# Turns of x and of attention weights by 32-row groups beside products, and two shared h buffers in PSUM

## The chip, the cores and the metric

The kernel runs on one core of one Trainium2 chip. The metric is the device time in microseconds of one execution, as the median of several runs. The core's engines are TensorE (PE; its weight loads are listed apart as PEld), VectorE (DVE), ScalarE (ACT), GpSimd (POOL) and SyncE (SP), whose queue issues all the DMAs of this kernel. All data are 32-bit floats. A "record" is one line of the hardware profiler: a 32-bit product on PE leaves two, a 32-bit transpose one.

## The reference

Four batches of 12608 tokens with 128 channels go through two attention steps with 32 inducing points, and then, token by token, through a block of 1024 hidden units:

```python
I = np.broadcast_to(inducing[None], (B, m, C))          # B, N, m, C = 4, 12608, 32, 128
def mab(q, kv):
    s = scale * (q @ kv.transpose(0, 2, 1))
    s = s - s.max(-1, keepdims=True)
    a = np.exp(s)
    a /= a.sum(-1, keepdims=True) + 1e-09
    return a @ kv
h = mab(I, x)                                           # 32 rows per batch
attn = mab(x, h)                                        # 12608 rows per batch
# then for the 50432 rows x of attn:
h = x @ w_in                                            # 128 -> 1024
sm = np.exp(h - h.max(-1)) / (sum + 1e-09)
solu = h * sm
ln = (solu - mu) / np.sqrt(var + 1e-06) * g_ln
out = ln @ w_out                                        # 1024 -> 128
```

## The kernel before

A tile is 128 tokens; a batch has 99 (the last one half full), so there are 396 tiles in all. The program is written out in full by a planner in Python: generators (`p1`, `p2`, `main`, `soft` and others) hand it operations with a cost and a priority, and `Planner.run` picks the next one among the engines by numbers of its own (`BEAT`, `SWITCH`, `AFTER`, `SLACK`, the `PR_` constants). Buffers are `Lock` objects: a generator asks for one and gets it when an earlier user has given it back. What reaches the chip is a fixed list of instructions per engine, with waits between them.

**First pass, `p1(b, k)`.** Nine groups per batch, seven of 12 tiles, one of 8 and one of 7. A group loads x into `xn`, turns each tile on PE (L561: full 128x128 transposes against the identity, four to an operation, into a PSUM bank), copies the four to `xT` on ACT (L547), stores `xT` to `xd` in DRAM, and then computes the scores against the inducing points (L589), a running maximum by way of a small product (L614), the exponentials (L639), and the weighted sum of x (L665). For batch 0 this pass runs alone, ahead of everything, in "early" buffers; for batches 1 to 3 it runs inside the main work of the batch before.

**`combine(b)`** ends the pass with the 32 rows h (L707, L714) and multiplies them with `w_in` into `hs` (L726, copied by ACT at L728), so that the hidden layer of a tile is a product of the 32 attention weights of each token with `hs`.

**Second pass, `p2(b, j)`.** It loads `xT` back, makes the scores against h (L768), the row maxima, the exponentials and the row sums, doubles the 32 weights of a token to 64 columns (`a4`), and turns `a4` on PE (L804: full transposes of two tiles each, four to an operation), copied to `aT` by ACT (L812).

**`main` and `soft`.** A tile's hidden layer takes eight products with 32 contraction rows (L902), two row groups of the PE array at a time, into a PSUM buffer `h` of two banks. DVE scales it by the row sums and takes the maximum (L940), which frees `h`; ACT takes the exponential (L950); POOL multiplies (L954); ACT squares (L965); DVE turns the result in 32x32 blocks (L978) into `vt`. Four tiles make a group for the output product.

**Products.** The output product of a group (L1023) is 128 matmuls, 32 for each of the four row groups of the array; row groups 0 and 1 are pair 0, which writes to buffer `op0`, and row groups 2 and 3 are pair 1 with `op1`. The function `beats` writes them in steps, called beats, of one step for each pair that has products ready. While `main` uses one pair for L902, it calls `beats` for the other pair, so that products of both kinds run side by side in the array. The full-array operations (L561, L804 and all the scores) are not mixed with products.

**PSUM.** Of the eight banks, `h` has two, the two `op` buffers two each, `tr` one (the turns of both passes and the scores of the second), `pb` one (the scores and sums of the first pass).

The weights `w_in` and `w_out` arrive as 64-bit numbers and are rounded by DVE, ACT and POOL (`weights_in`, `weights_out`) during the first pass of batch 0. `w_out` is then spread to `wc` by 16 DMAs (L481).

## Time and profile before

| | |
|---|---|
| median of 3 runs | 1289.62 us (1284.67 to 1293.36) |
| the profiled execution, its own time | 1285.68 us |
| its span, first to last instruction | 1283.9 us |
| busy: PE / DVE / ACT / POOL | 1246.2 / 1140.8 / 1140.1 / 1104.2 us |
| mean granted TensorE clock | 0.992 of full speed |
| L1023 products of the output | 25600 records |
| L902 products of the hidden layer | 6336 records |

The busy time of PE comes from records whose ends are modelled and overlap one another, so a stretch of PE that is 98% busy need not be at its peak. Where a stretch of PE is read below, it is by the starts of its records.

### The profile page before, as it was taken

Reading aid. Unit: us, or ns where it says so; the run is one execution under the profiler, and the core shown is the slowest. Engines: PE = TensorE matmul, PEld = TensorE weight load, DVE = VectorE, ACT = ScalarE, POOL = GpSimd, SP = SyncE. Lnnn points to the kernel's source line nnn. Section 1 sums busy time; section 2 is a strip of 40 time slices with the busy share of each in tenths; the row PEclk is TensorE's granted clock in tenths of the full one; section 3 lists DMA queues with packets and bytes.
Section 4 is the critical chain, followed back from the end, with each engine's and each line's share of the span. In section 5 each row is a group of like instructions: output and inputs, shape, how many; then the busy total and the mean of one; then the engine's idle time right before and its main releaser. Section 6 shows DMA issues by size and latency. Waiting matters only on the chain.

```text
span 1283.9 us, 75837 instructions
## 1 busy us (share of the span) xinstructions
PE 1246.2 (97%) x34221; PEld 1120.8 (87%) x34221; DVE 1140.8 (89%) x1825; ACT 1140.1 (89%) x2418; POOL 1104.2 (86%) x981
## 2 busy tenths in 40 slices
PE   8899999999999999999999999999999999999996
PEld 6689888889888888889888998888989999999996
DVE  5589989999898989999888999899999999999993
ACT  5489999999889989999789999989988999999993
POOL 2388988889889988988888997978889999999994
PEclk9999999999999999999899999999999999999998
DMA  9652333331232233332133134233021211111111
GB/s 361 188 164 70 111 103 94 93 111 43 77 117 60 78 102 119 103 109 74 28 102 94 43 103 138 91 101 102 21 82 54 58 55 53 54 38 43 29 29 41
DMA packets 118149, 113.46 MB, mean 88 GB/s; under 512 B 76577, under 2 KB 83777, under 8 KB 117697
## 3 DMA queue, kind: packets, MB, share of 16 engines
q1 hardware_dynamic: 117824, 108.62, 27.6%
q8 instruction: 267, 4.37, 1.4%
q14 instruction: 58, 0.47, 0.1%
HBM read 54.30 MB, written 52.18 MB: 83 GB/s over the span
## 4 chain that ended last, share of the span: by engine, by line
PE 70%; DVE 3%; ACT 2%; issue 1%; POOL 1%; POOLq 0%; DVEq 0%; ACTq 0%
PE op L1023 46%; PE h L902 15%; PE tr L561 2%; PE tr L804 2%; PE tr L768 1%; PE pb L665 1%; PE pb L589 1%; ACT sq L965 1%; DVE spare L940 1%; DVE vt L978 1%; ACT eu L950 1%; POOL eu L954 1%; PE pb L726 0%; DVE hn L940 0%; PE pb L614 0%
## 5 line engine op out<-in xcount | busy, mean ns | idle before, releaser
L1023 PE MATMUL op<-wc,vt 32*128 32x129 f32 x25600 | 1007.7, 275 | 12.5 <-issue 8.4
L1023 PEld LDWEIGHTS op<-wc,vt 32*128 32x128 f32 x25600 | 945.4, 185 | 54.3 <-issue 39.8
L902 PE MATMUL h<-hs,aT 32*128 32x128 f32 x6336 | 442.8, 277 | 3.2 <-DVE spare L940 1.2
L902 PEld LDWEIGHTS h<-hs,aT 32*128 32x128 f32 x6336 | 387.9, 187 | 32.1 <-DVE spare L940 6.2
L954 POOL TENSOR_TENSOR eu<-spare,eu 128x1024 f32<-128x1024 f32 x144 | 341.2, 2376 | 33.8 <-ACT eu L950 33.4
L954 POOL TENSOR_TENSOR eu<-hn,eu 128x1024 f32<-128x1024 f32 x140 | 331.8, 2376 | 25.1 <-ACT eu L950 24.3
L978 DVE STREAM_TRANSPOSE vt<-eu 128x1024 f32<-128x1024 f32 x284 | 349.2, 1233 | 1.1 <-POOL eu L954 0.9
L965 ACT ACTIVATE sq<-eu 128x1024 bf16<-128x1024 f32 x284 | 298.9, 1053 | 17.2 <-POOL eu L954 13.7
L940 DVE TENSOR_SCALAR_CACHE_REDUCE hn<-h,rn 128x1024 f32<-128x1024 f32 x198 | 252.1, 1273 | 38.8 <-PE h L902 30.6
L940 DVE TENSOR_SCALAR_CACHE_REDUCE spare<-h,rn 128x1024 f32<-128x1024 f32 x198 | 251.8, 1272 | 37.2 <-PE h L902 28.2
L950 ACT ACTIVATE eu<-hn,nm 128x1024 f32<-128x1024 f32 x140 | 160.3, 1145 | 19.9 <-DVE hn L940 19.0
L950 ACT ACTIVATE eu<-spare,nm 128x1024 f32<-128x1024 f32 x144 | 164.9, 1145 | 10.7 <-DVE spare L940 10.5
L954 POOL TENSOR_TENSOR spare<-hn,spare 128x1024 f32<-128x1024 f32 x58 | 137.5, 2374 | 15.6 <-ACT spare L950 15.5
L954 POOL TENSOR_TENSOR spare<-spare 128x1024 f32<-128x1024 f32 x54 | 128.0, 2373 | 16.9 <-ACT spare L950 16.4
L978 DVE STREAM_TRANSPOSE vt<-spare 128x1024 f32<-128x1024 f32 x112 | 138.2, 1235 | 0.0
L965 ACT ACTIVATE sq<-spare 128x1024 bf16<-128x1024 f32 x112 | 117.7, 1051 | 9.3 <-POOL spare L954 8.3
L1100 ACT ACTIVATE os<-spare,fin 128x128 f32<-128x128 f32 (+1 forms) x276 | 86.9, 391 | 1.5 <-POOL fin L1085 1.2
L950 ACT ACTIVATE spare<-hn,nm 128x1024 f32<-128x1024 f32 x58 | 66.4, 1145 | 6.7 <-DVE hn L940 6.4
L1045 DVE COPY spare<-op 128x258 f32<-128x258 f32 (+1 forms) x123 | 50.2, 416 | 24.6 <-PE op L1023 23.6
L950 ACT ACTIVATE spare<-spare,nm 128x1024 f32<-128x1024 f32 x54 | 61.9, 1146 | 6.5 <-DVE spare L940 6.5
L965 ACT ACTIVATION_READ_ACCUMULATOR sq<-eu 128x1 f32 x284 | 54.2, 191 | 0.0
L561 PE MATMUL tr<-ident,xn 128*128 128x128 f32 x297 | 48.8, 287 | 0.4 <-DMA xn<-in_x_dram 0.4
(180 smaller groups left out, 1028.0 us busy)
## 6 DMA issues: line engine op xcount, KB each, us to landing
out_dram<-os SPq DMA_DIRECT2D x96, 256.0 KB, 2.4
xT<-xd SPq DMA_DIRECT2D x27, 768.0 KB, 4.6
xn<-in_x_dram SPq DMA_DIRECT2D x22, 768.0 KB, 5.4
xd<-xT SPq DMA_DIRECT2D x21, 768.0 KB, 4.3
dl<-dd SPq DMA_DIRECT2D x396, 1.0 KB, 2.4
xd<-vt SPq DMA_DIRECT2D x7, 768.0 KB, 10.6
spare<-in_x_dram SPq DMA_DIRECT2D x5, 768.0 KB, 10.3
xT<-xd SPq DMA_DIRECT2D x5, 512.0 KB, 4.2
```

Of the source, the lines that this page charges most:

```text
L561: nc.tensor.transpose(out=tr[:, (s - c0) * P : (s - c0 + 1) * P], in_=xn[:, s, :], identity=ident)
L589: nc.tensor.matmul(sc[g * M : (g + 1) * M, : nn * M], lhsT=indT, rhs=xT[:, :nn, g * M : (g + 1) * M], start=True, stop=True)
L804: nc.tensor.transpose(out=tr[:h, (q - q0) * P : (q - q0 + 1) * P], in_=a4[:, q * P : q * P + h], identity=ident)
L902: nc.tensor.matmul(hp[:, cols], lhsT=aT[rows, i // 2, :], rhs=hs[rows, cols], start=True, stop=True)
L940: lambda: nc.vector.tensor_scalar(out=hn, in0=hp, scalar1=rn, scalar2=None, op0=ALU.mult, op1=ALU.min, accum_out=nm),
L950: "ACT", 1133, lambda: nc.scalar.activation(e, hn, AF.Exp, bias=nm, scale=-1.0, accum_out=G["S"][:, s : s + 1]), d, rel, srel,
L954: d = yield Op("POOL", 2330, lambda: nc.gpsimd.tensor_tensor(out=e, in0=hn, in1=e, op=ALU.mult), de, prio=t + PR_MU)
L965: "ACT", 1040, lambda: nc.scalar.activation(sq, e, AF.Square, scale=1.0 / 32.0, accum_out=G["qe"][:, s, 0:1]), d,
L978: lambda: nc.vector.transpose(out=G["vtb"][:, : n * FF].rearrange("p (j s t) -> p j s t", j=M, s=n)[:, :, s, :], in_=e.rearrange("p (a f) ...
L1023: nc.tensor.matmul(op[:rows, a - 2 * w, : C + 1], lhsT=vt[q, k, :], rhs=wc[q, k, :], start=(k == 0), stop=(k == JB - 1))
L1045: return lambda: eng(F["raw"][:rows, i0 : i0 + 2, :], op[:rows, :, : C + 1])
L1100: nc.scalar.activation(os[:rows, q, :], raw[:, q, :], AF.Copy, scale=y[:, i0 + q : i0 + q + 1])
```

## The change

Five things change together.

1. **The turns of x (in `p1` of batches 1 to 3) and of the attention weights (in `p2`, all batches)** are no longer full-array transposes. A new function `turned_rows` turns the 32 rows of one row group of a block at a time, `nc.tensor.transpose` of 32 rows by 128 columns into 128 rows by 32 columns, for the two row groups of one pair `w`; the second pair follows as an operation of its own. It goes through `beats`: three blocks, so six small turns, and beside them a step of products of the other pair, if that has any. The copies out of PSUM are now two of half the rows' columns each (L606, L885 in the new numbering), where they were one for every four blocks.
2. **PSUM.** There are two `h` buffers of two banks; `tr` and `pb` are gone. Everything that used those (`p1` of batches 1 to 3, `combine`, `p2`, the mean of `w_out`) asks for one of the two `h` buffers. `main` asks for `h` with the priority of its tile number less 30 (`H_LAST`). In `p1` the buffer of the scores goes back after the exponentials, and the weighted sums ask for one anew.
3. **The start.** The early pass of batch 0 has all eight banks as single buffers (four for turns, four for scores), and more buffers for x (the space of `wc` and both of `xn`). The `h` and `op` buffers come into being once the first pass of batch 0 and `hs` are done. The preparation of `w_out` may use `wc` only after that pass, and its mean (L466) asks for an `h` buffer.
4. **`combine`** of batches 1 to 3 makes the product with `w_in` in one operation of 1024 columns.
5. **The planner's numbers** change: `SWITCH` from 170 to 400 (a cost it puts on a full-array operation among products), `EAGER` from 60 to 120, the `AFTER` table (by 40 for nearly each pair of engines), priorities and starting tiles.

The first place is on PE in the middle of batch 0's main work. `tr` and `h_664` are where the turns go, `xn_71` and `xn_68` the tokens, `op_72`/`op_73` and `op_665`/`op_666` the two pairs' products, `h<-hs_124` the hidden layer. Before:

```order
L902 MATMUL h<-hs_124,aT_95 128x128 x2
L1023 MATMUL op_72<-wc,vt 128x129 x2
L902 MATMUL h<-hs_124,aT_95 128x128 x2
L1023 MATMUL op_72<-wc,vt 128x129 x2
L561 MATMUL tr<-ident,xn_71 128x128 x4
L1023 MATMUL op_72<-wc,vt 128x129 x2
L1023 MATMUL op_73<-wc,vt 128x129 x2
L1023 MATMUL op_72<-wc,vt 128x129 x2
```

Now:

```order
L1067 MATMUL op_666<-wc,vt 128x129 x2
L550 MATMUL h_664<-ident,xn_68 128x32 x6
L1067 MATMUL op_665<-wc,vt 128x129 x2
L550 MATMUL h_664<-ident,xn_68 128x32 x6
L1067 MATMUL op_665<-wc,vt 128x129 x2
L550 MATMUL h_664<-ident,xn_68 128x32 x6
L1067 MATMUL op_665<-wc,vt 128x129 x2
L550 MATMUL h_664<-ident,xn_68 128x32 x6
L1067 MATMUL op_665<-wc,vt 128x129 x4
```

The four full transposes that stood alone between products have become steps of six small ones, each followed by a step of the other pair's products; these four steps are one pair's half of a group of 12 tiles, and the other pair's half stands elsewhere.

The second place is the scores of the first pass on PE, which now go to one of the two `h` buffers (`h_663`) while `main` fills the other (`h_664`). Now:

```order
L1067 MATMUL op_666<-wc,vt 128x129 x2
L654 MATMUL h_663<-xT,indT 32x384 x4
L946 MATMUL h_664<-hs_123,aT_94 128x128 x2
L1067 MATMUL op_666<-wc,vt 128x129 x2
L946 MATMUL h_664<-hs_123,aT_94 128x128 x2
L1067 MATMUL op_666<-wc,vt 128x129 x2
L946 MATMUL h_664<-hs_123,aT_94 128x128 x2
L1067 MATMUL op_666<-wc,vt 128x129 x2
L946 MATMUL h_664<-hs_123,aT_94 128x128 x2
L1067 MATMUL op_666<-wc,vt 128x129 x2
```

Before, such scores (L589) went to `pb`, and all of `main` to the one `h`.

The third place is on PE at the end of the first pass of batch 0. `L714` makes the rows h, `L726` the product with `w_in`, `L768` the first scores of the second pass, `L804` the first turn of attention weights, `L902` the first tile of `main`. Before:

```order
L714 MATMUL h_e_78<-fold,accn 128x128
L768 MATMUL op_73<-xT_87,h_0_123 32x128 x4
L726 MATMUL pb<-w_in_sb,h_0_123 128x512
L726 MATMUL op_72<-w_in_sb,h_0_123 128x512
L804 MATMUL op_73<-ident,a_94 128x128 x2
L902 MATMUL h<-hs_124,aT_95 128x128 x8
```

Now, with the same steps at lines 785, 801, 844, 550 and 946:

```order
L785 MATMUL bank_e_74<-fold,accn 128x128
L801 MATMUL bank_e_75<-w_in_sb,h_0_122 128x512
L801 MATMUL bank_e_77<-w_in_sb,h_0_122 128x512
L844 MATMUL h_663<-xT_86,h_0_122 32x128 x4
L550 MATMUL h_663<-ident,a_93 128x32 x8
L946 MATMUL h_663<-hs_123,aT_94 128x128 x8
```

The first scores have moved from ahead of the two products with `w_in` to behind them.

The diff, cut to its core:

```diff
-EAGER = 60
-SWITCH = 170
+EAGER = 120
+SWITCH = 400
...
+H_LAST = -30
+TURNS = 3
+HN_MORE = 4
...
-    "PE": {"PE": 0, "ACT": 197, "DVE": 196, "POOL": 200, "SP": 250},
...
+    "PE": {"PE": 0, "ACT": 237, "DVE": 236, "POOL": 240, "SP": 290},
...
@@ weights_out
-        mp, rel = yield TRB
+        mp, rel = yield H
...
+        for k in range(NP):
+            yield p1_done[0][k]
+        o = yield Op("POOL", 200, lambda: nc.gpsimd.memset(wc[:, :, C : C + 1], 1.0), [d for e in p1_done[0] for d in e.after])
...
+    def turned_rows(tr, blocks, w, prio, *after):
+
+        def some(i):
+            for k, (block, h) in list(enumerate(blocks))[i * TURNS : (i + 1) * TURNS]:
+                for v in range(2):
+                    rows = slice((2 * w + v) * M, (2 * w + v + 1) * M)
+                    at = v * 512 + k * M
+                    nc.tensor.transpose(out=tr[:h, at : at + M], in_=block[rows, :h], identity=ident[rows, rows])
+
+        count = -(-len(blocks) // TURNS)
+        return Op("PE", count * BEAT, lambda: beats(count, (1 - w,), some), *after, prio=prio)
+
+    def in_rows(block, w):
+        return block.rearrange("p s (u v t) -> p s u v t", u=2, v=2)[:, :, w]
+
+    def from_rows(tr, n):
+        return tr.rearrange("p (v s t) -> p s v t", v=2, t=M)[:, :n]
...
@@ p1
-        lx, lt, ltr, lpb, lew = (EARLY_X, EARLY_T, EARLY_TR, EARLY_PB, EARLY_EW) if early else (XN, XT, TRB, PB, EW)
+        lx, lt, ltr, lpb, lew = (EARLY_X, EARLY_T, EARLY_TR, EARLY_PB, EARLY_EW) if early else (XN, XT, H, H, EW)
...
+                    nc.scalar.copy(in_rows(xT[:, :n, :], c0), from_rows(tr, n))
...
+        for w in () if early else range(2):
+            tr, trel = yield ltr
+            d = yield turned_rows(tr, [(xn[:, s, :], P) for s in range(n)], w, RUSH, [d for d, _ in xd], trel)
+            closing(d)
+            spawn(copy(w, None, tr, d), PRIO_P1(b, k))
...
+        if not early:
+            give(lpb, big, de)
+            big, rel = yield lpb
+        pooled = big[:, 512 - C : 512]
...
@@ p2
-        bank = EARLY_TR if b == 0 and j < ON_EARLY else TRB
+        bank = H
...
+        for w in range(2):
             tr, trel = yield bank
-            wide = min(P, (n - 2 * (q1 - 1)) * 2 * M)
...
+            blocks = [(a4[:, q * P : (q + 1) * P], P if q < nq - 1 else wide) for q in range(nq)]
+            dt = yield turned_rows(tr, blocks, w, None, dp, trel)
+            closing(dt)
...
@@ main
-            hp, rel = yield H
+            hp, rel = yield H.at(t + H_LAST)
...
@@ handover
+        d = yield hw_ready[0]
+        done += d
+        bank_pool.__exit__(None, None, None)
+        late = pool("late", 1, PSUM, side="right")
+        for i in range(2):
+            give(H, buf([P, FF], f"h{i}", where=late), *done)
+        for w in range(2):
+            give(OP[w], buf([P, 2, 512], f"op{w}", where=late), *done)
```

More of the change, by code (lines that the diff above doesn't have):

```diff
@@ L439, in weights_in @@
     def weights_in():
-        g = yield from rounded(w_in_sb, w_in.bitcast(U32), conv, None, conv_free, -18.5)
+        g = yield from rounded(w_in_sb, w_in.bitcast(U32), conv, None, conv_free, WIN)
         plan.set(w_in_ready, g)
@@ L492, in points @@
     def points():
+        tr_b, _ = yield EARLY_TR
         def warm():
@@ L501, in points, with beats, closing @@
         plan.set(ind_ready, d)
-        give(TRB, tr_b, d)
-        plan.scratch = (TRB, PB, H)
+        give(EARLY_TR, tr_b, d)
+        plan.scratch = (EARLY_TR, EARLY_PB)
+    stream = [dict(j=JB, emit=None, ready=0.0, close=None) for _ in range(2)]
+    flow = {"idle": Event(), "left": 2 * NB * NG, "prio": 0.0}
+    def beats(count, pairs=(0, 1), also=None):
+        for i in range(count):
+            if also:
+                also(i)
+            went = False
+            for w in pairs:
+                p = stream[w]
+                if p["j"] < JB and p["ready"] <= plan.now + i * BEAT + EAGER:
+                    p["emit"](2 * w, p["j"])
+                    p["emit"](2 * w + 1, p["j"])
+                    p["j"] += 1
+                    went = True
+            if not (went or also):
+                return i
+        return count
+    def closing(d):
+        for p in stream:
+            if p["close"] and p["j"] == JB:
+                close, p["close"] = p["close"], None
+                flow["left"] -= 1
+                close(d)
+    def turned_rows(tr, blocks, w, prio, *after):
[11 more added lines that the diff above has]
+        return tr.rearrange("p (v s t) -> p s v t", v=2, t=M)[:, :n]
     xT_dram = {}
@@ L1166, in handover @@
         give(XT, xT_b, *done)
+        for o in os_b:
+            give(OS, o, *done)
         give(EW, ew_b, *done)
```

216 lines of the change are left out of this document (90 added, 126 removed).

## The prediction, made before the changed kernel was run

> **What bounds the kernel now.** I read the page's busy times and its chain first, then the busy time by stretches, then single stretches of the timeline on PE.
>
> ```profile
> span 1283.9 us, 75837 instructions
> PE 70%; DVE 3%; ACT 2%; issue 1%; POOL 1%; POOLq 0%; DVEq 0%; ACTq 0%
> core 0: us, PE busy (x) PEld busy (x) DVE busy (x) ACT busy (x) POOL busy (x), PEclk, DMA share, GB/s
> 100.00:980.00 880.00, 864.10 (x24206) 771.78 (x24209) 807.51 (x1300) 807.96 (x1716) 776.40 (x680) 1.00 0.29 88
> 1100.00:1200.00 100.00, 98.50 (x2946) 93.53 (x2943) 95.13 (x133) 95.81 (x199) 97.95 (x85) 1.00 0.18 46
> ```
>
> Seven tenths of the chain is PE. From 100 to 980 us, where batches 0 to 2 are worked on and the first pass of the next batch runs beside them, PE is busy 98.2% (864.10 of 880), DVE and ACT 91.8% each, POOL 88.2%. From 1100 to 1200 us, in the last batch, no first pass is left, and POOL is the fullest after PE, with DVE and ACT at 95%. The same two stretches for the hidden layer's products alone (L902, 16 records a tile) give the pace:
>
> ```profile
> 100.00:980.00 880.00, 313.90 (x4531) 277.13 (x4532) 1.00 0.29 88
> 1100.00:1200.00 100.00, 41.11 (x590) 35.84 (x592) 1.00 0.18 46
> ```
>
> 4531/16 = 283 tiles in 880 us are 3.11 us a tile; 590/16 = 37 in 100 us are 2.71. DVE needs 807.51/283 = 2.85 us a tile in the first of them. So in the long stretch PE sets the pace, and DVE and ACT stand 8% behind it. That stretch is where the change can pay, up to what DVE and ACT allow.
>
> **What a full turn costs.** First the pace of products alone, and one block of four turns among them:
>
> ```profile
> 88.12 1.97 PE L1023 MATMUL op<-wc,vt 32*128 32x129 f32 x64
> 89.90 0.28 PE L902 MATMUL h<-hs,aT 32*128 32x128 f32 x2
> 93.94 1.07 PE L1023 MATMUL op<-wc,vt 32*128 32x129 f32 x32
> 94.94 0.66 PE L561 MATMUL tr<-ident,xn 128*128 128x128 f32 x4
> 95.53 0.50 PE L1023 MATMUL op<-wc,vt 32*128 32x129 f32 x8
> 8.06 1.53 PE L561 MATMUL op<-ident,spare 128*128 128x128 f32 x12
> ```
>
> 64 records, which are 8 beats of four row groups, run from 88.12 to 89.90: 0.2225 us a beat. The 32 records from 93.94 are 4 beats, so the next beat could have begun at 94.83. It begins at 95.53, 0.70 us late, and its 8 records take 0.50 where half a beat and one record (0.11 + 0.28) make 0.39, another 0.1. A block of four turns costs 0.80 us. Twelve turns take 1.53 and four 0.66, so a turn itself is 0.109, and of the 0.80 some 0.36 is spent going from products to turns and back. A block of two costs 0.80 - 2 x 0.109 = 0.58.
>
> **Turns removed.** The turns of both passes in the long stretch (the first row is L561, the second L804):
>
> ```profile
> 100.00:980.00 880.00, 44.90 (x273) 28.76 (x273) 1.00 0.29 88
> 100.00:980.00 880.00, 25.67 (x144) 14.70 (x144) 1.00 0.29 88
> ```
>
> 273 turns of x are 68 blocks: 68 x 0.80 = 55 us. The 144 turns of weights come six to a group of twelve tiles, as a block of four and one of two: 24 x 0.80 + 24 x 0.58 = 33 us. PE loses 88 us of work.
>
> **Turns added.** Each full turn becomes four small ones, six to a step: (273 + 144) x 4/6 = 278 steps, each on one pair while the other pair does a step of products, which has to be done anyway and fills half a beat (0.111 us). No row shows such a step. Its bounds come from the loads of the removed turns and from the one 32-row turn of the program:
>
> ```profile
> 85.86 0.14 PEld L561 LDWEIGHTS tr<-ident,xn 128*128 128x128 f32 x1
> 85.86 0.20 PEld L561 LDWEIGHTS tr<-ident,xn 128*128 128x128 f32 x2
> L499 PEld LDWEIGHTS tr<-ident,ind_sb x1: 135/135/135, 7.9 to 7.9; 32*128 32x128 f32 x1
> L561 PEld LDWEIGHTS tr<-ident,xn x297: 137/140/225, 73.5 to 941.5; 128*128 128x128 f32 x149
> ```
>
> A second load ends 0.06 us behind the first. A row group has three small turns in a step: if only the loads count, 0.18 us, hidden under the products' 0.2225; if load and stream (32 of 128 columns of 0.109 us, so 0.027) follow each other, 3 x 0.087 = 0.261. I take 0.24, the middle, since product records show load and stream side by side. Going in and out costs nothing, since the products beside it are of the same shape (32 rows by 128 columns). So 278 x (0.24 - 0.111) = 36 us. The page "TensorE: Matmul & The Clock Gate" of the Trainium skill (Part 1, on the 56 ns) says that starts of matmuls come no closer than about 25 ns, however short; a step of ten records (six turns, four of products) would then last an estimated 0.25 us, and the sum would be 39 us in place of 36; the densest row above, 64 records in 1.78 us, is 28 ns a record and does not decide it.
>
> Steps in which the other pair has nothing to do, or products go alone, waste half the array. Counted over the whole order of PE, beats with one pair alone are 394 before and 505 now; 111 x 0.111 = 12 us, some 9 of it in this stretch. PE's sum there is 864 - 88 + 36 + 9 = 821 us.
>
> **Copies and buffers.** ACT copied four blocks at a time; now two copies of 768 elements stand for three of 512:
>
> ```profile
> L547 ACT COPY xT<-tr 128x512 f32<-128x512 f32 (+1 forms) x75 | 42.8, 570 | 5.3 <-PE tr L561 5.0
> L1045 ACT COPY spare<-op 128x258 f32<-128x258 f32 (+1 forms) x77 | 27.1, 367 | 13.0 <-PE op L1023 12.8
> L787 ACT ACTIVATE a<-s 128x384 f32<-128x384 f32 (+3 forms) x37 | 18.2, 493 | 0.0
> L639 ACT ACTIVATE eT<-pb,small 128x384 f32<-128x384 f32 (+3 forms) x31 | 16.3, 527 | 0.0
> ```
>
> From 258 to 512 elements is 0.20 us, so 768 are 0.775, and 2 x 0.775 against 3 x 0.570 saves 0.16 a group, 4 us of ACT in the 25 groups of 27 that 273 of 297 turns are. Runs of 32 elements cost nothing extra: L787 writes such runs in 493 ns where L639 writes whole rows in 527. By the same two rows the copies of weights stay at 0.94 us a group (512 and 256 elements before, two of 384 now).
>
> One `h` buffer more helps DVE, whose idle time before L940 is a wait for it to be filled:
>
> ```profile
> DVE hn L940 <- PE h L902: 30.6, 73, 1.6
> DVE spare L940 <- PE h L902: 28.2, 66, 3.5
> POOL eu L954 <- ACT eu L950: 57.7, 64, 4.8
> ```
>
> In the first two rows 59 us of DVE's wait is there, and it shrinks when the next tile is already in the other buffer. The price is a new wait: scores and turns on PE ask for a buffer that DVE or ACT must first empty, and behind them in PE's queue stand the products of both kinds. In the order `main` has the other buffer while scores stand in one, as single-buffered as it is now.
>
> **The sum of the long stretch.** With PE at 821 us, DVE at 807.5 and ACT at 804 are as near. From 1100 to 1200 us DVE and ACT ran at 95.1 and 95.8%. At 95.5% DVE needs 846 us; PE would be 97% busy, less than the 98.2 it holds now. So 880 becomes 846: 34 us. If DVE runs at 97.5%, PE at its lower cost (0.2225 a step, 817 us) limits at 98.2%: 832, 48 us saved. If DVE gets only to 93%, 868, 12 us saved.
>
> **The ends.** At the start the second pass's first scores move behind the products with `w_in`:
>
> ```profile
> 43.30 2.19 PE L488 MATMUL tr<-ident 128*128 128x128 f32 x18
> 45.55 2.16 PE L488 MATMUL tr<-ident 128*128 128x128 f32 x18
> 52.73 0.42 PE L768 MATMUL op<-xT,h 128*32 128x128 f32 x8 [1.36 <-DVE h L716]
> 53.09 1.13 PE L726 MATMUL pb<-w_in_sb,h 128*128 128x512 f32 x2
> 55.46 0.44 PE L804 MATMUL op<-ident,a 128*128 128x128 f32 x2 [0.38 <-POOL a L788]
> 56.35 1.16 PE L902 MATMUL h<-hs,aT 32*128 32x128 f32 x16 [0.46 <-ACT aT L812]
> 26.72 2.20 SPq L357 DMA_DIRECT2D spare<-in_x_dram  x3
> L481 SPq DMA_DIRECT2D wc<-hn x16: 591/622/771, 52.5 to 63.9; - x16
> ```
>
> Now the time from 53.09 to 55.46 lies ahead of the scores: 2.4 us later. Against it, the last x loads, which SP issues at 26.72 between stores, come ahead of all the stores, and the preparation of `w_out` leaves the first pass; PE fills its waits there with dummy turns (2.19 and 2.16 us), and some 4 of that can go. I take 2 us saved, with 3 lost and 5 saved as ends. The 16 spreads of `wc`, from 52.5 to 63.9 us now, come behind two tiles of `main`, some 10 us later; the products that wait for them have room, since `vt` holds three groups of four tiles, so I charge nothing (4 us if that cover is short).
>
> The end was PE alone:
>
> ```profile
> 1253.40 20.70 PE op L1023 x644
> ```
>
> Behind the last product of the hidden layer the order has 108 beats of output products where it had 82, at 0.2225 us 5.8 us more; the last hidden product comes earlier for it, as the second buffer lets `main` run ahead. I charge 2 us, with 0 and 6 as ends. In the last batch PE gains little, since POOL is at 98%: 1 us.
>
> Total: 34 + 2 - 2 + 1 = 35 us off the profiled execution's 1285.68, which lies 4 us under the median of 1289.62. That makes 1251 by the profiled one and 1255 by the median; I forecast 1252, nearer the one whose rows I read.
>
> **Rivals.** *The buffers stall `main`.* While scores hold one buffer, `main` fills the other for two tiles, and needs it emptied between.
>
> ```profile
> 55.93 0.37 ACT L812 COPY aT<-op 128x256 f32<-128x256 f32 x1
> 57.56 1.28 DVE L940 TENSOR_SCALAR_CACHE_REDUCE hn<-h,rn 128x1024 f32<-128x1024 f32 x1 [1.55 <-PE h L902]
> 58.77 0.08 DVE L940 DVE_READ_ACCUMULATOR hn<-h,rn 128x1 f32 x1
> 67.21 1.24 DVE L978 STREAM_TRANSPOSE vt<-eu 128x1024 f32<-128x1024 f32 x1
> ```
>
> Filling takes 1.16 us (L902 at 56.35), DVE begins 0.05 behind its end and is done 1.29 later, and PE began 0.05 behind ACT's copy (56.30 to 56.35): 2.55 us, or 3.79 if DVE has just begun a transpose of 1.24. From 2.85 us a tile, DVE's need, it decides. At 3.79, 0.94 us x 2 tiles x 25 groups are 47 us, more than all that is gained: 1299. For it: both buffers are lent to turns, scores and sums alike. Against it: one buffer alone runs 2.71 us a tile from 1100 to 1200 us.
>
> *The small turns run one after the other.* If a row group's next load starts only when its last turn has gone through, a step is 3 x (0.135 + 0.027) = 0.49 us (L499's load and the stream above): 278 x 0.38 = 106 us for 36, so PE has 891 us, at 98.2% a stretch of 907, 27 us more than now: 1313. It decides from about 0.39 us a step, where 278 steps eat the 43 us that PE gains net. For it: the change makes four loads of each one, and 32 rows load in 135 ns where 128 take 140. The Trainium skill has the same ("TensorE: Matmul & The Clock Gate", Part 2, on LDWEIGHTS: a load takes as long as it has columns, however few its rows), and these two rows agree. Against it: the second load above ends 0.06 us behind the first.
>
> *DVE and ACT hold the pace.* If what keeps them at 92% is the chain of hand-overs between the engines, not PE, the stretch stays at 868 to 880, and with 1 us at the ends the time is 1273 to 1285 by the profiled execution, 1279 as the middle. For it: POOL's wait of 57.7 us for ACT's exponentials (the third row of waits above), which no turn on PE makes. Against it: 95% in the last batch, with the same chain.
>
> **Chances.** Forecast 0.68, its own range 1230 to 1275 (48 saved in the stretch and 6 at the ends; 12 and a loss of 1). Pace held 0.16, half of it faster by over 1% (13 us, about what can be told from no change), half not. Buffers 0.08, of it 0.03 slower. Small turns 0.08. Faster 0.68 + 0.08 = 0.76; same 0.08 + 0.05 = 0.13; slower 0.03 + 0.08 = 0.11. The range from 1228 to 1288 takes in the forecast and the pace held, and leaves out the two slow rivals.
>
> **What would show it.** Right: L550 with some 2000 records and steps near 0.24 us beside products; DVE and ACT at 95% from 100 us on; a pace near 2.95 us a tile; DVE's wait before its scaling step well under 59 us. Wrong: runs of small turns with 0.4 us a step, PE records of the hidden layer that wait for DVE or ACT by tens of us, or engines that stay at 92% while PE's own starts thin out.

## The result: 1252.5 us, and the profile after

The changed kernel takes 1252.54 us (median of 4 runs, 1248.87 to 1254.37) against 1289.64 us before (median of 4, 1284.67 to 1293.36). The ratio is 0.9718, with a 95% interval from 0.9696 to 0.9740. The profiled execution of after took 1254.37 us with a span of 1252.6; against the profiled one of before (1285.68 and 1283.9) that is 31.3 us less.

The busy time by stretches comes first (columns: PE, weight loads, DVE, ACT, POOL with their busy us and instruction counts, granted clock, DMA). The first stretch ends where tile 297 begins, the first tile of the last batch: at 946.9 us now, at 979.9 us before, which is where the prediction's stretch ended too.

```profile
core 0: us, PE busy (x) PEld busy (x) DVE busy (x) ACT busy (x) POOL busy (x), PEclk, DMA share, GB/s
100.00:946.90 846.90, 828.12 (x25289) 766.23 (x25284) 789.29 (x1284) 786.22 (x1671) 765.98 (x672) 1.00 0.30 91
1100.00:1200.00 100.00, 96.73 (x3103) 94.04 (x3098) 94.66 (x134) 97.56 (x213) 98.33 (x86) 1.00 0.15 38
```

The same stretches of after for the hidden layer's products alone (L946):

```profile
100.00:946.90 846.90, 308.34 (x4513) 276.90 (x4514) 1.00 0.30 91
1100.00:1200.00 100.00, 40.06 (x608) 36.46 (x608) 1.00 0.15 38
```

4513/16 = 282 tiles in 846.9 us are 3.00 us a tile, where before took 3.11. PE is busy 97.8% of the stretch (98.2 before), DVE 93.2 and ACT 92.8 (91.8 both). From 1100 to 1200 us POOL is still the fullest, at 98.3%.

The groups of instructions of after, with their shapes kept apart (x count, busy us, mean ns, idle before):

```profile
L550 PE MATMUL h<-ident,xn 32*128 32x32 f32 x1188 | 46.1, 220 | 1.6 <-issue 1.0 <-ACT xT L606 0.4
L550 PE MATMUL h<-ident,a 32*128 32x32 f32 x784 | 36.7, 222 | 5.6 <-POOL a L864 3.9 <-ACT aT L885 1.1 <-DVE spare L984 0.5
L606 ACT COPY xT<-h 128x768 f32<-128x768 f32 x42 | 33.0, 786 | 5.5 <-PE h L550 5.4
L885 ACT COPY aT<-h 128x384 f32<-128x384 f32 x54 | 25.3, 468 | 7.9 <-PE h L550 7.9
```

One group of small turns on PE's timeline of after (start, length, count):

```profile
119.98 0.26 PE L550 MATMUL h<-ident,xn 32*128 32x32 f32 x4
120.04 0.28 PE L1067 MATMUL op<-wc,vt 32*128 32x129 f32 x2
120.07 0.29 PE L550 MATMUL h<-ident,xn 32*128 32x32 f32 x4
120.15 0.28 PE L1067 MATMUL op<-wc,vt 32*128 32x129 f32 x2
...
120.63 0.23 PE L550 MATMUL h<-ident,xn 32*128 32x32 f32 x2
120.69 1.53 PE L1067 MATMUL op<-wc,vt 32*128 32x129 f32 x46
```

24 turns, four steps, run from 119.98 to 120.69: 0.18 us a step. Beside them the other pair's products go on in their own time, two records each 0.11 us.

The waits of after that answer to those of before:

```profile
POOL eu L998 <- ACT eu L994: 55.6, 47, 3.5
PE op L1067 <- issue: 16.8, 15, 2.5
DVE spare L984 <- PE h L946: 15.8, 25, 2.5
DVE hn L984 <- PE h L946: 11.8, 14, 3.3
```

DVE waits for the hidden layer for 27.6 us in place of 58.8. POOL's wait for the exponentials has hardly moved (57.7 before). The second row has doubled: PE stands still for 16.8 us with nothing in the profile that releases it, where before it did so for 8.4:

```profile
PE op L1023 <- issue: 8.4, 8, 1.7
```

For what follows, PE's records between the first and the last hidden product are split into three: *excursions*, from the last product record before full-array work to the first one after it; *stops*, where two records of products or small turns that follow each other start 0.3 us or more apart (what such a gap has over the usual 0.028 us counts); and the rest, *products and small turns in a row*. The starts are from the trace; us throughout, the last column is the median of the timed runs, the others are of the profiled one.

| kernel | first hidden product at | excursions | products, small turns | stops | last hidden product to end of span | median |
|---|---|---|---|---|---|---|
| before | 56.4 | 220.7 | 955.6 | 20.5 | 30.8 | 1289.6 |
| after | 52.2 | 115.5 | 1002.3 | 42.3 | 40.4 | 1252.5 |
| e1_whole_turns | 53.0 | 218.9 | 981.9 | 17.8 | 41.2 | 1316.0 |
| e2_own_h | 58.7 | 177.3 | 1035.0 | 68.0 | 24.8 | 1363.5 |
| e3_turns_alone | 52.1 | 114.8 | 1032.6 | 36.2 | 40.5 | 1280.0 |
| e4_old_numbers | 63.4 | 120.5 | 1038.3 | 74.6 | 34.5 | 1331.5 |
| e5_before_new_numbers | 59.1 | 257.1 | 972.9 | 34.8 | 27.3 | 1351.9 |
| e6_short_xT | 52.2 | 115.4 | 999.6 | 28.4 | 40.1 | 1237.0 |
| e8_beat224 | 52.5 | 116.0 | 1002.5 | 37.1 | 39.8 | 1242.0 |
| e9_six | 52.2 | 119.1 | 1019.8 | 34.4 | 39.4 | 1266.7 |
| e10_before_short_xT | 56.3 | 219.4 | 952.8 | 16.4 | 30.8 | 1278.8 |
| e11_three_pieces | 52.1 | 116.1 | 999.3 | 37.4 | 39.6 | 1243.6 |
| e12_old_handover | 53.2 | 117.1 | 1016.2 | 41.8 | 39.2 | 1271.4 |
| e14_both | 52.8 | 116.0 | 999.8 | 33.2 | 39.9 | 1242.4 |

From before to after: the excursions fall by 105.2 us, products and small turns in a row take 46.7 more, the stops 21.8 more, the start gives 4.2, the end takes 9.6. Together 31.3 us less. Of the 105.2 us, 8.7 are not the change of the turns: between 61 and 76 us the kernel before fills waits of PE with 59 dummy turns, and after has none there.

The rows were timed on several chips. Before, timed again beside them, has medians from 1286.5 to 1291.4 us, so a difference of 4 us or less between two rows of the last column says little.

### The profile page after: what moved, and what is told of

Its sections match the earlier page's. It is cut to its first block, busy times and chain, and to the rows that moved or that the text cites. A ratio compares the mean times of both kernels' runs of the same rounds, so it can differ in the third digit from the quotient of the medians.

```text
span 1252.6 us, 78887 instructions
## 1 busy us (share of the span) xinstructions
PE 1200.5 (96%) x35640; PEld 1113.4 (89%) x35640; DVE 1124.9 (90%) x1816; ACT 1127.9 (90%) x2414; POOL 1101.9 (88%) x981
## 3 DMA queue, kind: packets, MB, share of 16 engines
q8 instruction: 279, 4.57, 1.5%
## 5 line engine op out<-in xcount | busy, mean ns | idle before, releaser
L1067 PE MATMUL op<-wc,vt 32*128 32x129 f32 x25600 | 1034.2, 275 | 22.9 <-issue 16.8
L998 POOL TENSOR_TENSOR eu<-spare,eu 128x1024 f32<-128x1024 f32 x191 | 452.3, 2374 | 33.1 <-ACT eu L994 30.7
L946 PE MATMUL h<-hs,aT 32*128 32x128 f32 x6336 | 436.5, 277 | 4.9 <-DVE spare L984 1.4
L1022 DVE STREAM_TRANSPOSE vt<-eu 128x1024 f32<-128x1024 f32 x330 | 403.9, 1232 | 7.1 <-POOL eu L998 7.1
L946 PEld LDWEIGHTS h<-hs,aT 32*128 32x128 f32 x6336 | 392.2, 189 | 19.1 <-issue 4.4
L1009 ACT ACTIVATE sq<-eu 128x1024 bf16<-128x1024 f32 x330 | 346.7, 1051 | 25.4 <-POOL eu L998 20.9
L998 POOL TENSOR_TENSOR eu<-hn,eu 128x1024 f32<-128x1024 f32 x139 | 329.4, 2373 | 25.3 <-ACT eu L994 24.8
L994 ACT ACTIVATE eu<-spare,nm 128x1024 f32<-128x1024 f32 x191 | 217.8, 1141 | 2.9 <-DVE spare L984 2.9
L1144 ACT ACTIVATE os<-spare,fin 128x128 f32<-128x128 f32 x272 | 85.5, 390 | 5.1 <-DMA out_dram<-os 3.6
L1022 DVE STREAM_TRANSPOSE vt<-spare 128x1024 f32<-128x1024 f32 x66 | 81.1, 1229 | 0.9 <-POOL spare L998 0.8
L1009 ACT ACTIVATE sq<-spare 128x1024 bf16<-128x1024 f32 x66 | 69.4, 1052 | 6.9 <-POOL spare L998 6.0
L998 POOL TENSOR_TENSOR spare<-hn,spare 128x1024 f32<-128x1024 f32 x30 | 71.2, 2372 | 2.5 <-ACT spare L994 2.3
L550 PE MATMUL h<-ident,xn 32*128 32x32 f32 x1188 | 46.1, 220 | 1.6 <-issue 1.0
L550 PEld LDWEIGHTS h<-ident,xn 32*128 32x128 f32 x1188 | 44.4, 137 | 2.4 <-issue 1.2
## 6 DMA issues: line engine op xcount, KB each, us to landing
xT<-xd SPq DMA_DIRECT2D x27, 768.0 KB, 4.9
xn<-in_x_dram SPq DMA_DIRECT2D x21, 768.0 KB, 5.4
xd<-xT SPq DMA_DIRECT2D x21, 768.0 KB, 4.1
xd<-vt SPq DMA_DIRECT2D x7, 768.0 KB, 11.5
spare<-in_x_dram SPq DMA_DIRECT2D x5, 768.0 KB, 12.8
```

What stands on the lines that cost most here:

```text
L550: nc.tensor.transpose(out=tr[:h, at : at + M], in_=block[rows, :h], identity=ident[rows, rows])
L946: nc.tensor.matmul(hp[:, cols], lhsT=aT[rows, i // 2, :], rhs=hs[rows, cols], start=True, stop=True)
L994: "ACT", 1133, lambda: nc.scalar.activation(e, hn, AF.Exp, bias=nm, scale=-1.0, accum_out=G["S"][:, s : s + 1]), d, rel, srel,
L998: d = yield Op("POOL", 2330, lambda: nc.gpsimd.tensor_tensor(out=e, in0=hn, in1=e, op=ALU.mult), de, prio=t + PR_MU)
L1009: "ACT", 1040, lambda: nc.scalar.activation(sq, e, AF.Square, scale=1.0 / 32.0, accum_out=G["qe"][:, s, 0:1]), d,
L1022: lambda: nc.vector.transpose(out=G["vtb"][:, : n * FF].rearrange("p (j s t) -> p j s t", j=M, s=n)[:, :, s, :], in_=e.rearrange("p (a f) ...
```

## The experiments

Theory A: PE set the pace, and the gain is what it no longer spends on going from products to whole turns and back, and on turns with nothing beside them. Rival B: the gain is the second `h` buffer that DVE finds filled. Rival C, which the prediction did not name: the gain is the planner's new numbers, and the turns are incidental.

### Whole turns again

```diff
-            d = yield turned_rows(tr, [(xn[:, s, :], P) for s in range(n)], w, RUSH, [d for d, _ in xd], trel)
+            c0, c1 = (0, -(-n // 2)) if w == 0 else (-(-n // 2), n)
+            def whole():
+                for s in range(c0, c1):
+                    nc.tensor.transpose(out=tr[:, (s - c0) * P : (s - c0 + 1) * P], in_=xn[:, s, :], identity=ident)
+            d = yield Op("PE", SWITCH + 108.7 * (c1 - c0), whole, [d for d, _ in xd], trel, prio=RUSH)
```

(and the same for the weights, three pairs to a half.)

> The kernel after, with the turns of the first pass of batches 1 to 3 and of the second pass as whole 128x128 blocks again, in two halves per group (6 and 6 tiles of x, 3 and 3 pairs of weights), so that the number of copies, the buffers and the planner's numbers stay those of after. Theory A (the gain is what PE no longer spends on going from products to whole turns and back, and on turns with nothing beside them): PE gets back about 140 blocks at some 0.36 us of switching and 0.109 us a turn, about 46 us net of the small steps taken away; it has some 3% of room in the long stretch, so the time rises by 25 to 35 us, to 1278 to 1288 us. Rival B (the gain is the second h buffer that DVE finds filled) and rival C (the gain is the planner's new numbers) both expect the time of after within 5 us.

Measured: 1316.0 us, 63 more than after and 27 more than before (ratio to before 1.0208, interval 1.0187 to 1.0228). The row of its long stretch and two of its blocks on PE:

```profile
100.00:1000.70 900.70, 894.83 (x24241) 805.08 (x24237) 802.20 (x1286) 806.85 (x1711) 759.58 (x668) 1.00 0.28 86
```

```profile
127.06 0.28 PE L1077 MATMUL op<-wc,vt 32*128 32x129 f32 x2
127.26 0.87 PE L617 MATMUL h<-ident,xn 128*128 128x128 f32 x6
128.06 1.50 PE L1077 MATMUL op<-wc,vt 32*128 32x129 f32 x38
...
135.10 0.55 PE L884 MATMUL h<-ident,a 128*128 128x128 f32 x3
135.58 1.84 PE L1077 MATMUL op<-wc,vt 32*128 32x129 f32 x56
```

PE is at 99.4% there, the clearest sign that it is the bound. By the table the whole turns cost 103.4 us of excursions, of which 20.4 come back as beats that are no longer spent beside small turns and 24.5 as stops that PE's longer work covers. My 25 to 35 us was too low at two places: I put the net cost at 46 us, where these terms leave 58.5, and I let 3% of free room on PE swallow part of it. B and C expected no change: both are wrong as sole causes. That it is slower than before too comes from the products: between the first and the last hidden product they take 26.3 us more than before, and 10.4 us more come behind it, as in its order products go alone more often.

### Small turns with nothing beside them

```diff
-        return Op("PE", count * BEAT, lambda: beats(count, (1 - w,), some), *after, prio=prio)
+        return Op("PE", count * BEAT, lambda: beats(count, (), some), *after, prio=prio)
```

> The kernel after, with nothing beside the small turns: the other pair's products that ran in the same steps are put off to their own beats. The small turns, their buffers and the planner's numbers stay. If the partner's products are what a step costs anyway (theory A), the 278 steps lose half a beat of 0.111 us each, 31 us of PE, of which some 15 to 25 us reach the end: 1268 to 1278 us. If the gain is the switches alone, not the sharing of the array, the time stays within 5 us of after. Rivals B and C expect no change beyond 5 us either.

Measured: 1280.0 us, 27.5 more than after (ratio to before 0.9927, 0.9906 to 0.9947). On its timeline 24 turns run from 116.87 to 117.59, 0.18 us a step, as fast as beside products:

```profile
116.87 0.88 PE L550 MATMUL h<-ident,xn 32*128 32x32 f32 x24
117.59 1.83 PE L1067 MATMUL op<-wc,vt 32*128 32x129 f32 x40
```

Products and small turns in a row take 30.3 us more, the 31 expected, and nearly all of it reaches the end, 2 us more than A's range allowed. So sharing the array is worth 27.5 us of the 63 that separate after from whole turns; the rest is the switch and the turns' own time.

### One buffer for the hidden layer, one for all else

```diff
@@ combine
+        if b:
+            yield p1_done[b][NP - 1]
...
@@ main
-            hp, rel = yield H.at(t + H_LAST)
+            hp, rel = yield HM
...
```

(The first edit lets `combine` of batches 1 to 3 ask for a buffer only when the whole first pass has ended.)

> The kernel after, with the two h buffers kept apart: the hidden layer of main always takes the one, and scores, small turns, sums and the rest all take the other, so main is single-buffered as it was before. Theory A expects the small turns to keep nearly all of the gain: within 8 us of after. Rival B (the second buffer lets DVE find the next tile filled) expects DVE's wait before its scaling step to go back from 28 us toward 59, and 20 to 30 us of the gain to go: 1272 to 1282 us.

Measured: 1363.5 us, far above what either expected, and above before.

```profile
POOL eu L1000 <- ACT eu L996: 135.8, 140, 3.1
DVE spare L986 <- PE h L948: 48.9, 78, 2.3
DVE hn L986 <- PE h L948: 35.7, 54, 2.3
```

DVE waits 84.6 us for the hidden layer, more than the 58.8 of before, and the table has 68 us of stops and 62 us more of excursions than after (52 of them dummy turns with which PE fills waits that the planner foresaw). Before had a buffer of its own for turns; here scores, turns and sums queue for a single one. So the run doesn't undo one part of the change: it is poorer than both kernels. It shows that, with these numbers, one buffer for all else is too few. How much of the 37 us the second buffer gives by itself stays open.

### The planner's numbers, each way round

```diff
-EAGER = 120
-SWITCH = 400
+EAGER = 60
+SWITCH = 170
...
-PR_EX = 1
-PR_EV = -20
+PR_EX = -2
+PR_EV = -60
...
-    "PE": {"PE": 0, "ACT": 237, "DVE": 236, "POOL": 240, "SP": 290},
+    "PE": {"PE": 0, "ACT": 197, "DVE": 196, "POOL": 200, "SP": 250},
```

(after with before's numbers; the kernel before got the opposite. `LATE` and `WOUT`, which place the preparation of `w_out`, stayed as they were. One number that changed, `HN_MORE`, is not the planner's: it says how many of the spare buffers serve as `hn` and not as `eu`.)

> The kernel after, with the planner's numbers of before wherever both kernels have them (priorities, slacks, due times and the lengths that the planner assumes). Small turns and shared h buffers stay. Its order of PE has 4455 beats where after has 4419, 36 x 0.2225 = 8 us more. Theory A (the gain is the turns) expects 1252 to 1266 us. Rival C (the gain is the new numbers) expects 25 us or more of the gain to go: 1278 us or more. A shuffle of the plan alone moved the time by 10 us, so less than that says nothing.

> The kernel before, with the planner's numbers of after. Whole turns and the three buffers of before stay. Its order has 4237 beats where before has 4189 (48 x 0.2225 = 11 us more) and 265 stretches of other work where before has 237 (28 x 0.36 = 10 us more). Theory A expects no gain, and a time from 1285 to 1312 us. Rival C expects most of the gain to appear here: 1255 to 1270 us.

Measured: small turns with the old numbers 1331.5 us (ratio 1.0333, 1.0302 to 1.0365), whole turns with the new numbers 1351.9 us (1.0492, 1.0459 to 1.0525). Each half of the change alone is slower than before by 3 to 5%; only both are faster. A's range was wrong by 65 us for the first and by 40 for the second, C's by 80 for the second; only C's 1278 us or more for the first held. So the gain is neither the turns' alone nor the numbers'. The waits of after with the old numbers:

```profile
DVE spare L984 <- PE h L946: 24.8, 31, 2.2
DVE hn L984 <- PE h L946: 20.1, 28, 3.1
PE op L1067 <- DVE vt L1022: 11.9, 19, 1.6
PE h L946 <- DVE hn L984: 9.0, 11, 1.5
PE h L946 <- DVE spare L984: 8.7, 13, 1.4
```

PE's matmuls wait 29.6 us for DVE, where the same three rows of after sum to 5.0 (2.9, 0.7, 1.4). By the table the 78.6 us between the two spans are: 11.2 a later first hidden product, 5.0 excursions, 36.0 products, 32.3 stops, and 5.9 less at the end. Of the products 8 us are the 36 beats more. The rest goes along with a lower granted clock, 0.96 in the first row below where after has 1.00. Between the first and the last hidden product the clock stands at half for 106 us in this kernel and for 30 in after, which is 38 us of full speed lost. The two longest stretches at half begin at 395.9 and 727.0 us and last 27.3 us each; the second row lies in the first of them, the third right behind it:

```profile
100.00:950.00 850.00, 810.59 (x23487) 748.41 (x23484) 741.67 (x1198) 742.70 (x1551) 717.03 (x628) 0.96 0.27 82
396.00:423.00 27.00, 22.88 (x252) 19.34 (x252) 18.94 (x28) 18.54 (x34) 19.69 (x13) 0.50 0.20 66
423.30:440.00 16.70, 16.13 (x564) 15.66 (x564) 16.45 (x24) 16.06 (x30) 16.05 (x11) 1.00 0.33 99
```

PE leaves 252 records in 27 us there and 564 in the 16.7 us behind. That is little more than a quarter of the rate, so PE waits in that stretch as well.

In the kernel before with the new numbers the largest term is 36.4 us of excursions, most of it dummy turns: PE fills 238 into `tr` where it filled 83.

```profile
L488 PE MATMUL tr<-ident 128*128 128x128 f32 x238 | 31.0, 285 | 3.0 <-DVE hn L469 1.3 <-DVE s L775 1.1 <-ACT aT L812 0.7
```

One part of the numbers alone, the table of hand-over times:

> The kernel after, with only the planner's table of hand-over times (what it adds between an instruction on one engine and the one on another that needs it) as it was before; the table of after has 40 ns more for every hand-over that ends or begins another engine's work. All of before's numbers together cost 79 us. If the table is what does it, most of that shows here: 1290 us or more, with waits of PE for DVE and ACT of 30 us and more. If it is the numbers on the passes' start and priority, 1252 to 1265 us: its order has 4427 beats, 8 more than after, 2 us.

Measured: 1271.4 us, 18.9 more than after (0.9852, 0.9822 to 0.9883), between the two expectations. 13.9 us of the 14.9 between the spans stand in the products, none in the stops; 2 us are the 8 beats more, and some 8 go along with the clock, which stands at half for 45 us between the first and the last hidden product where after has 30. It is a quarter of what all the numbers cost; the other 60 us belong to the rest (starts and priorities of the passes, slacks, the length planned for a switch) or to their going together, and weren't taken apart further.

### How far a shuffle moves the time

```diff
-BEAT = 225
+BEAT = 224
```

> The kernel after, with one of the planner's numbers changed that should not matter: a beat is planned at 224 ns in place of 225. The plan comes out a little different everywhere. It gauges how far the time moves by such a shuffle alone: all theories expect 1252 us within 5 us; if it moves by 10 us or more, differences of that size between the other runs say nothing about a cause.

Measured: 1242.0 us (0.9639, 0.9597 to 0.9681), 10.5 us faster than after; the intervals of the two ratios don't meet. All theories were wrong here: a planner's number moved by half a per cent is worth ten microseconds. Its four runs lie far apart, from 1236.7 to 1249.8 us, with the profiled one at the top; so the spans differ by 4.6 us only, and the table has 5.2 us less of stops. Between kernels whose plans differ, 10 us say nothing on a cause: the 27, 63, 79 and 111 us of the other runs stand clear of that, the 18.9 of the hand-over table hardly. Runs that leave the order of PE as it is have no new plan, but they too can move transfers against one another.

### Twice as many turns to a step

```diff
-TURNS = 3
+TURNS = 6
```

> The kernel after, with twelve small turns to a step in place of six (a row group has six of them beside one step of products). Rows of after show a row group starting a small turn every 0.062 us where turns run in a row, so three fit under the 0.2225 us of the products beside them and six take 0.37. The order has 62 beats fewer (14 us), and about 170 steps that last 0.15 us longer (25 us): theory A expects 5 to 15 us more than after. If a row group is not held to that rate beside products, 10 us less.

Measured: 1266.7 us, 14 more (0.9826, 0.9798 to 0.9854), inside A's 5 to 15, though not far above what a shuffle does. Its products and small turns take 17.5 us more with 62 beats fewer, as is to be expected if six turns of a row group outlast the products beside them and three don't. Some 8.5 us of it go along with the clock (47 us at half between the first and the last hidden product, 30 in after).

### The stops of PE

The longest stop of after, on PE, with the releaser in brackets:

```profile
670.58 0.54 PE L1067 MATMUL op<-wc,vt 32*96 32x129 f32 x10
673.57 1.02 PE L1067 MATMUL op<-wc,vt 32*96 32x129 f32 x22 [2.45 <-issue]
```

Ahead of it SP had issued two loads of 768 KB behind each other:

```profile
665.79 0.38 SPq L829 DMA_DIRECT2D xT<-xd  x1
666.26 0.38 SPq L361 DMA_DIRECT2D xn<-in_x_dram  x1
```

The DMA view of after for the 8 us before the loads, the 8 us with them, and the 8 us behind (packets, MB, share of the 16 engines; queue 8 brings instructions in pieces of 16 KB). Over the span it brings 279 pieces, 4.57 MB, which is 64 bytes for each of the 71280 records of PE and its weight loads; the other queue of instructions brings 0.48 MB. So queue 8 is read as PE's own:

```profile
q8 instruction: 2, 0.03, 1.6%
q1 hardware_dynamic: 186, 0.00, 1.3%
...
q1 hardware_dynamic: 969, 1.39, 55.9%
q8 instruction: 1, 0.02, 0.9%
...
q1 hardware_dynamic: 143, 0.40, 13.0%
q8 instruction: 3, 0.05, 2.2%
```

Between 100 and 950 us these fetches start every 4.0 us in the median (198 of them; before 183, every 4.3 us). One started at 663.22, the next at 671.08, 7.9 us later, and PE stood still from 670.86 on. The six longest stops of that stretch, at 487.1, 649.3, 670.9, 749.6, 768.0 and 808.7 us, all begin within 0.5 us of a fetch that came 6.1 to 8.0 us behind the one before, and in all six PE goes on 2.2 to 2.6 us after that fetch began. A late fetch alone is not enough: of the 12 in that stretch that came 6 us or more behind the one before, five have no stop of 0.3 us behind them. To try it, the loads of the second pass were shortened:

```diff
-            lambda: nc.sync.dma_start(xT[:, :n, :].rearrange("p s t -> p (s t)"), xT_dram[b][:, s0 * P : (s0 + n) * P]),
+            lambda: nc.sync.dma_start(xT[:, : (n if (b, j) < (0, 3) else 2), :].rearrange("p s t -> p (s t)"), xT_dram[b][:, s0 * P : (s0 + (n if (b, j) < (0, 3) else 2)) * P]),
```

> The kernel after, instruction for instruction in the same order, but the second pass's loads of the turned x (all but the first three of batch 0) fetch 2 tiles of up to 12, so that 768 KB become 128 KB; what is left out is the rest of that load, nothing else. If PE's stops of 1 to 2.7 us (15 of them, 16.8 us, with no releaser in the profile) come from its instruction fetches waiting behind two big loads, they go: PE's wait without a releaser falls from 16.8 to under 6 us, and the time by 8 to 14 us. If they have another cause (the order of PE, a wait the profile misses), the time stays within 4 us of after and the stops stay where they were.

Measured: 1237.0 us, 15.5 less than after, a little more than expected, with no instruction in another place (0.9604, 0.9576 to 0.9632). Its wait of PE without a releaser, and its stretch up to tile 297:

```profile
PE op L1067 <- issue: 5.4, 8, 1.3
```

```profile
100.00:931.30 831.30, 821.62 (x25276) 761.32 (x25276) 788.54 (x1284) 784.91 (x1670) 765.14 (x672) 1.00 0.25 74
```

The wait falls from 16.8 to 5.4 us, as expected, and DVE is at 94.9% of the stretch, ACT at 94.4. The same edit in the kernel before:

> The kernel before, instruction for instruction in the same order on PE, DVE, ACT and POOL, with the second pass's loads of the turned x cut to 2 tiles of up to 12 (all but the first three of batch 0); what is left out is the rest of those loads. The same cut took 15.5 us from the kernel after. If the stops behind big loads are as dear in both kernels, before falls by 12 us or more, to 1278 us or less, and they explain nothing of the shortfall of the gain. If they are dearer in after, because its PE is fed more instructions in the same time, before falls by 3 to 9 us (its PE waits without a releaser for 8.4 us where after has 16.8), and 6 to 12 us of the gain were lost there.

Measured: 1278.8 us (0.9908, 0.9879 to 0.9938), 12.6 less than its own before. By the medians the loads cost after 15.5 us and before 12.6, too near to tell apart; from tile 0 to tile 297 the profiles have 15.7 and 7.2. So the first expectation came by the medians and the second by the profiles, and which holds stays open. Without that part of the loads the change saves 41.8 us by the medians (1278.8 to 1237.0), with it 37.1; by the ratios to each one's own before it is 39 and 36. Before's wait without a releaser fell only from 8.4 to 6.0 us. By the table its 8.3 us between the spans are 4.1 of stops, 2.8 of products and 1.3 of excursions, so about half came by another way, which wasn't followed.

The last question is whether bytes or packets delay a fetch:

```diff
+            lambda: [
+                nc.sync.dma_start(xT[:, i : min(i + 4, n), :].rearrange("p s t -> p (s t)"), xT_dram[b][:, (s0 + i) * P : (s0 + min(i + 4, n)) * P])
+                for i in range(0, n, 4)
+            ],
```

> The kernel after, with each of the second pass's loads of the turned x issued as up to three loads of 4 tiles, one behind the other: the same bytes, but 2 KB to a partition's packet in place of 6 KB. If an instruction fetch waits for the bytes queued ahead of it, nothing changes: within 4 us of after, and PE's wait without a releaser stays near 17 us. If it waits for a few large packets at a time, that wait falls below 10 us and the time by 6 to 15 us.

Measured: 1243.6 us (0.9634, 0.9602 to 0.9666), 8.9 less, with the wait without a releaser at 10.7 us. The time is what smaller packets were to bring, the wait lies between the two expectations, and a stop of 3.1 us at 764.0 us is longer than any of after. The waits without a releaser of all of PE's lines fell by less, from 18.6 to 14.3 us, and the beat of 224 alone has them at 12.5. So the gain of the pieces is no larger than a shuffle's, and why they help is not settled.

Both edits that helped together:

> The kernel after with both edits that made it faster, the beat planned at 224 ns and the loads of the turned x in pieces of 4 tiles. Alone the first gave 1242.0 us and the second 1243.6 us against 1252.5. If they work on different waits their 10 and 9 us add up: about 1233 us. If both do no more than move the loads away from the moments in which PE's next instructions are fetched, or the 224 is chance, the second adds little: 1238 to 1246 us.

Measured: 1242.4 us (0.9641, 0.9597 to 0.9686): they don't add up, as the second expectation had it. Three versions lie at 1242 to 1244 us, below after and before.

## Why the prediction was right

**The bound.** Right for before. For after I had DVE and ACT as the limit, at 95.5%, and PE at 97%. PE stands at 97.8% and DVE at 93.2, so it is PE that sets the pace still: the kernel with whole turns put it at 99.4% and lost 63 us, and the one with shorter loads took some of its stops away and gained 15.5.

**Turns removed.** I took 88 us off PE in the long stretch; the last batch's nine groups at 1.38 us make it about 100 in all. The excursions fell by 105.2, of which 96.5 are left without the dummy turns of before.

**Turns added.** 0.24 us a step was a little too much. A row group starts a turn each 0.062 us, so three take 0.18 to 0.19 and stay under the products' 0.2225; what a step costs is the products' time. The order has 230 beats more than before, 230 x 0.2225 = 51.2 us; the table has 46.7, and behind the last hidden product 205 more output records stand (863 for 658), 5.7 us. What the sum did not have is the clock: between the first and the last hidden product it stands at half for 30 us, 14 before, so some 8 us of full speed are lost. Between 119.98 and 120.69 us, 36 records start, 20 ns each, and the two turns of a pair start 6 to 11 ns apart on their row groups. The Trainium skill's floor of 25 ns between starts ("TensorE: Matmul & The Clock Gate", Part 1), which would have given an estimated 0.25 us a step, is not borne out across row groups by these starts. The serial rival, at 0.49 us a step, is excluded by the same rows, at 0.18.

**Copies.** 0.786 us for 768 elements where I had 0.775, and 0.936 for two of 384 where I had 0.94.

**The pace of DVE and ACT.** This is the term that was off. I had them at 95.5% and the stretch at 846 us. From tile 0 to tile 297 before takes 923.5 us (first row below) and after 894.7 (second row): 28.8 saved, not 34, with DVE at 93.2% from 100 us on.

```profile
56.35:979.90 923.55, 906.26 (x24968) 807.05 (x24972) 842.48 (x1352) 840.84 (x1778) 809.53 (x702) 0.99 0.30 92
```

```profile
52.17:946.90 894.73, 870.57 (x26069) 803.65 (x26072) 826.50 (x1340) 822.32 (x1743) 802.19 (x697) 0.98 0.31 94
```

What stood in the way is not in the sum: PE's stops, 21.8 us more of them. With the loads shortened DVE reaches 94.9% and the same way takes 879.0 us. So most of the missing 2% is lost where loads hold up PE, in the profiles; the medians bear out less of it. That the stretch still came out near 846 us (846.9 from 100 us on) has a second reason that I missed: I held DVE's work at 807.5 us, by which 93.2% makes 866 us and 14 saved. DVE's work between the two tiles fell from 842.5 to 826.5 us instead. Half of that is no saving: 289 of the tiles' transposes stand ahead of tile 297 where before had 294, 8 us. Another 3 us are the scaling step, at 1264 ns where it took 1272. So less work of DVE partly made up for its lower level, which is luck.

**The ends.** The start gave 4.2 us where I had 2. In the last batch 7.9 us went (273.2 to 265.3 from tile 297 to the last hidden product) where I had 1, but 5.7 of them are the output products that now run behind it. Behind it, 9.6 us came where I had 2: 6.4 up to the last output product (20.7 before, 27.1 after), most of it those 5.7, and 3.1 between that and the end (10.1 before, 13.2 after). I had let an earlier last hidden product pay for the beats behind it, and booked the two in different lines. The two lines together are 1.7 us more, where they had 1 more in the forecast. (The slow end of my own range, a loss of 1, does not follow from the ends I gave: 3 lost, 6 charged and 1 gained make a loss of 8, and 1282 us.) POOL's last long multiplication ends at the same distance from the end in both kernels, 23.6 us in the first row (before) and 22.7 in the second (after):

```profile
1257.91 2.37 POOL L954 TENSOR_TENSOR eu<-hn,eu 128x1024 f32<-128x1024 f32 x1
```

```profile
1227.54 2.37 POOL L998 TENSOR_TENSOR eu<-hn,eu 128x1024 f32<-128x1024 f32 x1
```

**The sum.** 4.2 + 28.8 - 1.7 = 31.3 us by the profiled executions, where I had 35: 1251 forecast by the profiled one, 1254.37 taken. The medians are 37.1 apart, since the profiled execution of before lay 4 us under its median and that of after 2 us above. So 1252 came out closer to the median than its terms are to theirs. With a shuffle of the plan worth 10 us, a hit within 1 us is luck; what the forecast earned is the direction and the size of the gain.

**The rivals.** Buffers that stall `main`: in after PE waits 0.7 and 1.4 us for DVE's scaling, so it didn't happen. The kernel with one buffer apart, where PE waits 16.8 us for the scaling and DVE 84.6 for PE, shows what too few buffers can cost, more than my 1299. Pace held by DVE and ACT: POOL's wait for the exponentials did stay (55.6 us), and DVE and ACT rose only from 91.8 to 93%, short of the 95% that I named as a sign of being right. But the stretch from 100 us on fell to 846.9 us where this rival had 868 to 880, so it didn't hold the pace.

**What I left out.** I read the plan's beats and took the plan itself as given. The runs show that it isn't a detail: the same small turns under the old numbers are 79 us slower. The prediction was right with the new numbers because the order that I counted was made by them.

## What to carry to other kernels

Where four row groups of the array can work apart, a little work of the same shape beside the products costs no more than the products' time (three turns of a row group to a step here; six cost more), and a block that needs the whole array costs the way in and out (some 0.36 us here); count both in blocks, and count the steps in which half the array stands idle. A plan made by numbers belongs to its structure: test a structural change with numbers fitted to it, and take a difference of one per cent between two plans for chance until another plan shows it too. When an engine stops and nothing in the profile releases it, look at the queue that brings its instructions and at the large transfers issued just before.

## What was not expected of the hardware

PE's longest stops go with 16 KB of instructions that come late: in after the fetches start every 4.0 us, and behind two loads of 768 KB one came 7.9 us behind the last, with 2.45 us of standstill. Shortening one of the two, the load of the turned x, took PE's unexplained wait from 16.8 to 5.4 us and the time down by 15.5 us. So that the loads have a part in the stops is shown; by which rule the queues are served, and why some late fetches pass without a stop, is not.

The granted clock is either full or half in all these traces. In the kernel with the old numbers it stood at half for 27.3 us from 395.9 us on (the row stands above). In the long stretch of after it did so twice, for 3.4 us each, from 771.6 and from 812.6 us, which a mean of 1.00 hides. Both begin 1 to 2 us behind a stop, of 2.28 us that ended at 770.5 and of 1.94 us that ended at 810.9:

```profile
771.70:775.00 3.30, 3.30 (x69) 3.30 (x65) 2.57 (x4) 0.48 (x1) 1.58 (x1) 0.50 0.03 1
```

The longest stop, of 2.45 us, has none behind it, so the length of a stop doesn't decide alone. In the kernel with shorter loads, whose waits without a releaser are at most 1.3 us long, the clock is full from 100 to 950 us. So a plan with more stops of PE seems to pay twice, for the stops and in its products' pace; that the stops lower the clock was not tried by itself.
